# Column tiles or the full array for the dense matmuls behind the last attention times V

## The chip, the cores and the metric

The kernel runs on one core of one Trainium2 chip. The metric is the device time of one execution in microseconds, and the median of several runs is compared. The engines of the core are named as the profile names them: PE (TensorE, the matmuls; PEld are its weight loads), DVE (VectorE), ACT (ScalarE), POOL (GpSimd) and SP (SyncE, which issues the transfers).

## The reference

The input x has 2048 tokens of 512 features, in bf16. Two branches are computed from it and mixed by a gate per token.

- Branch A is attention in segments with a memory: 32 heads of 16 features, 4 segments of 512 tokens. Within a segment it is causal softmax attention. Beside that, each segment reads a memory matrix and a normaliser that the earlier segments have filled with phi(k) times v, where phi(t) is t + 1 for positive t and exp(t) otherwise. Both parts are mixed by a sigmoid per head, and the result is multiplied by wo.
- Branch B is a gated feed-forward layer: relu(x W_gate) times (x W_up), 1792 wide, times W_down.
- The output is g a + (1 - g) b, where g is a sigmoid of the sum of x times gate_w.

Cut to what matters here:

```
q, k, v = x @ wq, x @ wk, x @ wv          # heads of 16, segments of 512
o = g_h * memory(q) + (1 - g_h) * softmax(q k^T / 4 + mask) v
a = o @ wo
h = relu(x @ W_gate) * (x @ W_up)          # 2048 x 1792
b = h @ W_down
out = g * a + (1 - g) * b
```

## The kernel before

**How the work is tiled.** A segment is 512 tokens. Activations lie transposed in SBUF, features on the 128 partitions and the 512 tokens of a segment along the free axis. Per segment the kernel does four chunks each of q and k (proj_q, proj_k), four of v (proj_v), the scores and their exponentials (visit), the masks, attention times V (in attention), the read of the memory (dens and recall) and its update (memory), and the feed-forward layer (ffn_tasks): 14 chunks of gate and up, whose product is kept in 14 tiles hT, and then four output tiles of 128 tokens each (out_tile). An output tile gathers in one PSUM bank 14 matmuls of hT times wd_sb and 4 matmuls of oT times wo_sb. oT is the attention result, transposed. DVE multiplies the bank by a column ngcol into osr (line 958), and SP issues the transfer to the output (line 966).

**The last output tile** (tt = 15) is cut in three parts of columns: 256, 128 and 128 wide, each with its own 18 matmuls, its own eviction and a bank of its own. The first two parts take banks 7 or 6 (OBANKS), the third bank 5 or 4. The first part is written out alone, the other two together.

**Two ways to use the array.** The attention matmuls have small operands and use parts of the array. A score matmul contracts over 32 rows; these tasks have mode "row" (line 683). Attention times V, the denominators and the memory update write 32 output rows; they have mode "col" (lines 755, 812 and 878) and issue four matmuls that lie side by side in the array's columns. The read of the memory uses 32 by 32 tiles, mode "quad" (line 853). The dense matmuls (projections, feed-forward, output) have no mode. They contract over 128 rows and write 128, and full() can issue each of them in two ways:

```
if not col:
    nc.tensor.matmul(out, lhsT=lhsT, rhs=rhs, start=start, stop=stop)      # line 491
    return
for j in range(4):                                                       # line 495, four times
    r = slice(32 * j, 32 * j + 32)
    nc.tensor.matmul(out[r], lhsT=lhsT[:, r], rhs=rhs, ..., tile_position=(0, 32 * j))
```

A dense task has up to two matmuls (GM = 2). Its field flex holds their number if the matmul is wider than 128 columns, and 0 otherwise. So the dense tasks of the 128-wide parts of the last output tile can never be column-tiled, since their flex is 0.

**What sets the order.** Every operation is a task of a plan. The list ORDER, written out in the file, gives the order in which all tasks are issued, and UNITS gives the buffer that each takes. The plan's dependencies are only looked at by an assertion, that a task stands behind those it depends on. The waits between engines come from the tiles that the instructions read and write. Each engine works off its own instructions in the order of the list.

**Which way a dense task goes** is set in Plan.run by settle(). The PE tasks between two row or quad tasks make a stretch. If there is a col task anywhere in the stretch, all dense tasks of it with flex over 0 are column-tiled; if there is none, all use the full array. The last stretch of the program begins behind the last scores. It holds the last two attention times V tasks, the last gate and up chunks of segment 3 and all matmuls of the output tiles 12 to 15.

Of the kernel before, what the change touches and what calls it, by code (L numbers as in the profile page):

```python
# [12 lines left out]
P = 128  # L13
# [5 lines left out]
NSEG = 4  # L19
# [111 lines left out]
class Plan:  # L131
# [19 lines left out]
    def run(self):  # L151
        order = [self.tasks[int(n)] for n in ORDER.split()]
        slots = {}
        for t in self.tasks:
            for s in t.need + t.frees:
                slots.setdefault(id(s), s)
        assert len(order) == len(set(map(id, order))) == len(self.tasks)
        assert len(slots) == len(UNITS)
        for s, n in zip(slots.values(), UNITS):
            s.units = s.cands[int(n, 36)]  # L160
        for t in self.tasks:
            for s in t.frees:
                s.left += 1
        stretch, held, done = [], set(), set()

        def settle():
            col = any(t.mode == "col" for t in stretch)
            for t in stretch:
                t.col = bool(t.flex) and col
            stretch.clear()  # L170
        for t in order:
            assert all(d.n in done for d, off in t.deps if off % 1 != 0.25)
            done.add(t.n)
            for s in t.need:
                assert not held & set(s.units)
                held |= set(s.units)
            if t.eng == "PE":
                if t.mode in ("row", "quad"):
                    settle()
                else:  # L180
                    stretch.append(t)
            for s in t.frees:
                s.left -= 1
                if s.left == 0:
                    held -= set(s.units)
        settle()
        return order


@with_exitstack  # L190
def kernel(
# [71 lines left out]
    def bank(slot):  # L263
        return ps[:, slot.i * L:(slot.i + 1) * L]
# [165 lines left out]
    att, prj, ffn, xread, x0_first = {}, {}, {}, [], []  # L430
# [58 lines left out]
    def full(out, lhsT, rhs, start, stop, col):  # L489
        if not col:  # L490
            nc.tensor.matmul(out, lhsT=lhsT, rhs=rhs, start=start, stop=stop)  # L491
            return
        for j in range(4):
            r = slice(32 * j, 32 * j + 32)
            nc.tensor.matmul(out[r], lhsT=lhsT[:, r], rhs=rhs, start=start, stop=stop,  # L495
                             tile_position=(0, 32 * j))

    def matmuls(key, deps, sl, ops, start=True, stop=True, prev=None, width=L, need=(), chunk={}, at=0):
        n = len(ops)
        for k in range(0, n, GM):  # L500
            def emit(col=False, k=k):
                for q in range(k, min(k + GM, n)):
                    lhsT, rhs = ops[q]()
                    full(bank(sl)[:, at:at + width], lhsT, rhs, start and q == 0,
                         stop and q == n - 1, col)
            first = prev is None
            m = min(k + GM, n) - k
            t = plan.add("PE", (width / 2.4 + 2.5) * m, key - (0 if first else CONT), emit,
                         list(deps) + [d for q in range(k, k + m) for d in chunk.get(q, ())],
                         PEL, need=[sl] + list(need) if first else (),  # L510
                         flex=m if width > P else 0, size=2 * m)
            if not first:
                t.deps.append((prev, 0.0))
            prev, deps = t, ()
        return prev
# [397 lines left out]
    def ffn_tasks(seg):  # L913
        plan.tag = "gu"
        i = seg % 2
        hs = []
        for fv in range(NF):
            key = K(4 * seg + FLAG + fv * 4.0 / 18)
            gsl, usl, rs, hs1 = work(), work(), plan.one("rgr"), plan.one("hT")
            piece = next(k for k, (a, b) in enumerate(FP) if a <= fv * P < b)  # L920
            g = matmuls(key, xin(seg) + [got_g[piece]], gsl, proj_mm(wg_sb, fv, seg),
                        need=[rs])
            r = plan.add("ACT", 478, key - RL, lambda sl=gsl, rs=rs: nc.scalar.activation(  # L923
                rgr[rs.i][:], bank(sl), ACT.Relu), [g], ACL, frees=[gsl])
            u = matmuls(key + 1, xin(seg) + [got_u[piece]], usl, proj_mm(wu_sb, fv, seg),
                        need=[hs1])
            xread.extend((g, u))
            hs.append((plan.add("DVE", 605, key - RL, lambda sl=usl, rs=rs, hs1=hs1: (
                nc.vector.tensor_tensor(hT[hs1.i][:], bank(sl), rgr[rs.i][:], ALU.mult)),  # L929
                [r, u], DVL, frees=[usl, rs]), hs1))  # L930
        for qb in range(4):
            tt = 4 * seg + qb
            key = K(4 * seg + FLAG + (14 + qb) * 4.0 / 18)
            parts = [[(0, D)]]
            if tt == NT - 1:
                parts = [[(0, 2 * P)], [(2 * P, 3 * P), (3 * P, D)]]
            for cols in parts:
                out_tile(seg, i, hs, key, qb * P, tt, cols)

    def out_tile(seg, i, hs, key, lc, tt, cols):  # L940
        plan.tag = "down"
        os, b, c0 = plan.one("osr"), [], cols[0][0]
        for n0, n1 in cols:
            w = n1 - n0
            sl = plan.one("ps", [HOST] if tt < 12 else OBANKS if n0 < 3 * P else (5, 4))
            prev, mine = None, []
            for f0, f1 in ((0, 5), (5, 10), (10, 14)):
                prev = matmuls(key, [h[0] for h in hs[f0:f1]] + got_d[0:2 if f0 < 5 else 4]
                               + [att["ot", 4 * seg + c] for c in range(OTW)], sl, [
                    lambda fv=fv, n0=n0, n1=n1: (hT[hs[fv][1].i][:, lc:lc + P], wd_sb[:, fv, n0:n1])  # L950
                    for fv in range(f0, f1)], start=(f0 == 0), stop=False, prev=prev, width=w)
                prev.frees += tuple(h[1] for h in hs[f0:f1])
                mine.append(prev)
            a = matmuls(key, got_o + [att["ot", 4 * seg + c] for c in range(NC)], sl, [
                lambda ci=ci, n0=n0, n1=n1: (oT[i][:, ci, lc:lc + P], wo_sb[:, ci, n0:n1])
                for ci in range(NC)], start=False, prev=prev, width=w)
            b.append(plan.add("DVE", 95 + 1.12 * w, key - RL, lambda sl=sl, n0=n0, n1=n1: (
                nc.vector.tensor_scalar(osr[os.i][:, n0 - c0:n1 - c0], bank(sl)[:, 0:n1 - n0],  # L958
                                        ngcol[:, tt:tt + 1], None, ALU.mult)),
                [a, att["ng", seg]] + b, DVL, need=[] if b else [os], frees=[sl]))  # L960
            if tt < 12:
                first = mine[0].deps[-1][0].deps[-1][0]
                hosts.append((first, a))
        ffn["o", seg, tt % 4] = a
        c1 = cols[-1][1]
        plan.add("SP", 400, key, lambda: nc.sync.dma_start(
            out=outf[tt * P:(tt + 1) * P, c0:c1], in_=osr[os.i][:, 0:c1 - c0]), b[-1:],
            1400 if tt == NT - 1 else 2400, frees=[os], xfer=400.0)
# [101 lines left out]
```

## Time and profile before

| what | value |
|---|---|
| median of 3 runs | 263.6 us (263.37 to 263.92) |
| the profiled execution's own time | 262.86 us |
| its span, first to last instruction | 261.1 us |
| PE busy | 257.4 us, 4137 matmuls |
| DVE, ACT, POOL busy | 202.1, 182.9, 67.3 us |
| mean granted TensorE clock | 1.0 of full |

The profile shows one execution. Its page gives the busy time of each engine and the chain of work that ended last. The timeline lists instructions in order of time, neighbours of one line, operation and tiles merged into a row: start, length, engine, line, operation, written and read tiles, array rows by array columns used, moving columns, and the count. Matmuls overlap in the array, so the length of a row holds the drain of its last matmul, and the difference between the starts of two rows is what the first costs the stream. Shapes of a merged row are those of its first instruction.

### The profile page before, as it was taken

What the parts mean: (1) busy time and instruction counts of PE and PEld (TensorE: products, weight loads), DVE (VectorE), ACT (ScalarE), POOL (GpSimd) and SP (SyncE); (2) the same over time, 40 slices, a digit from 0 to 9 for tenths busy, and PEclk for the clock granted to TensorE, in tenths of its full rate; (3) what the DMA queues carried; (4) which work ended last, traced back from release to release, by engine and by line L of the source; (5) the groups of instructions that cost most, each with busy time, mean ns of one, the idle gap of its engine ahead of it and who ended that gap; (6) DMA issues with size and microseconds to landing.
All of it is one profiled execution on the core that took longest, in us unless ns stands there. A gap on an engine that the chain in (4) does not pass through costs nothing.

```text
span 261.1 us, 9476 instructions
## 1 busy us (share of the span) xinstructions
PE 257.4 (99%) x4137; PEld 120.3 (46%) x4137; DVE 202.1 (77%) x452; ACT 182.9 (70%) x186; POOL 67.3 (26%) x188
## 2 busy tenths in 40 slices
PE   8999999999999999999999999999999999999995
PEld 3434444445445544444545444444445544455443
DVE  1699889998979957998998874887988736586521
ACT  2299899999889668888296848999278856891000
POOL 8028651423313113121030423123022322111000
DMA  7999881120006335000026440000000043000011
GB/s 186 335 290 259 264 195 48 19 62 3 3 25 151 104 52 125 18 3 3 15 55 120 138 143 20 4 3 15 4 1 13 20 147 92 0 3 5 3 43 40
DMA packets 31601, 19.76 MB, mean 76 GB/s; under 512 B 16072, under 2 KB 30024, under 8 KB 31560
## 3 DMA queue, kind: packets, MB, share of 16 engines
q1 hardware_dynamic: 31144, 18.90, 28.1%
q8 instruction: 32, 0.52, 0.8%
q10 hardware_dynamic: 416, 0.26, 0.3%
q14 instruction: 9, 0.07, 0.1%
HBM read 13.21 MB, written 2.55 MB: 60 GB/s over the span
## 4 chain that ended last, share of the span: by engine, by line
PE 98%; ACT 0%; DVE 0%; issue 0%
PE ps L491 50%; PE ps L495 30%; PE ps L683 9%; PE ps L755 7%; PE ps L1003 1%; PE ps L878 1%; PE ps L853 0%; PE ps L812 0%; PE ps L529 0%; ACT xT L544 0%; DVE osr L958 0%
## 5 line engine op out<-in xcount | busy, mean ns | idle before, releaser
L712 ACT ACTIVATE E<-ps 128x2048 bf16<-128x2048 f32 (+3 forms) x79 | 120.4, 1552 | 26.4 <-PE ps L683 25.6
L728 POOL TENSOR_SCALAR_AFFINE_SELECT E<-E 128x256 bf16<-128x256 bf16 x128 | 53.7, 448 | 155.0 <-ACT E L712 149.1
L929 DVE TENSOR_TENSOR hT<-ps,rgr 128x512 bf16<-128x512 f32 x56 | 37.8, 681 | 21.9 <-PE ps L491 13.6
L923 ACT ACTIVATE rgr<-ps 128x512 bf16<-128x512 f32 x56 | 32.7, 597 | 20.4 <-PE ps L495 8.9
L491 PE MATMUL ps<-xT,wu_sb 128*128 128x512 bf16 x164 | 43.0, 380 | 0.0
L491 PE MATMUL ps<-xT,wg_sb 128*128 128x512 bf16 x136 | 35.5, 380 | 0.0
L495 PE MATMUL ps<-wd_sb,hT 128*32 128x512 bf16 (+1 forms) x572 | 33.9, 369 | 0.0
L683 PE MATMUL ps<-QT,KT 32*128 32x64 bf16 (+3 forms) x768 | 27.8, 244 | 0.0
L786 DVE STREAM_TRANSPOSE T<-ps 128x512 f32<-128x512 f32 x32 | 21.9, 700 | 3.6 <-PE ps L755 3.2
L495 PE MATMUL ps<-xT,wg_sb 128*32 128x512 bf16 x352 | 23.7, 380 | 0.0
L491 PEld LDWEIGHTS <-wu_sb 128*128 128x128 bf16 x164 | 14.9, 98 | 18.5 <-issue 2.5
L491 PE MATMUL ps<-wd_sb,hT 128*128 128x512 bf16 (+1 forms) x109 | 23.0, 340 | 0.0
L683 PEld LDWEIGHTS <-KT 32*128 32x128 bf16 x768 | 11.0, 92 | 24.2 <-issue 22.9
L958 DVE TENSOR_SCALAR osr<-ps,ngcol 128x512 bf16<-128x512 f32 (+2 forms) x18 | 12.3, 682 | 12.5 <-PE ps L495 9.7
L491 PEld LDWEIGHTS <-wg_sb 128*128 128x128 bf16 x136 | 12.7, 98 | 15.7 <-issue 1.3
L495 PEld LDWEIGHTS <-hT 128*32 128x32 bf16 x572 | 14.0, 97 | 13.0 <-issue 1.3
L755 PE MATMUL ps<-E,Vp 128*17 128x320 bf16 (+3 forms) x512 | 19.1, 273 | 0.0
L712 ACT ACTIVATE Em<-ps 128x2048 bf16<-128x2048 f32 (+2 forms) x11 | 15.6, 1415 | 4.3 <-PE ps L683 4.1
L495 PE MATMUL ps<-xT,wu_sb 128*32 128x512 bf16 x240 | 16.2, 379 | 0.0
L491 PE MATMUL ps<-wv_sb,xT 128*128 128x512 bf16 x58 | 14.7, 380 | 0.0
L586 DVE CAST QT<-ps 128x512 bf16<-128x512 f32 x16 | 10.8, 683 | 4.9 <-PE ps L491 4.5
L491 PE MATMUL ps<-xT,wk_sb 128*128 128x512 bf16 x52 | 14.0, 380 | 0.0
(100 smaller groups left out, 306.9 us busy)
## 6 DMA issues: line engine op xcount, KB each, us to landing
out_dram<-osr SPq DMA_DIRECT2D x15, 128.0 KB
xn<-in_A_x_dram SPq DMA_DIRECT2D x3, 512.0 KB
xn<-coefs SPq DMA_DIRECT2D x6, 256.0 KB
cdr<-coefs SPq DMA_DIRECT2D x6, 256.0 KB
wg_sb<-in_B_W_gate_dram SPq DMA_DIRECT2D x2, 512.0 KB
wu_sb<-in_B_W_up_dram SPq DMA_DIRECT2D x2, 512.0 KB
wd_sb<-in_B_W_down_dram SPq DMA_DIRECT2D x2, 512.0 KB
wg_sb<-in_B_W_gate_dram SPq DMA_DIRECT2D x2, 384.0 KB
```

The costliest lines, as they stand in the source:

```text
L491: nc.tensor.matmul(out, lhsT=lhsT, rhs=rhs, start=start, stop=stop)
L495: nc.tensor.matmul(out[r], lhsT=lhsT[:, r], rhs=rhs, start=start, stop=stop, tile_position=(0, 32 * j))
L586: prj["q", seg, c] = plan.add("DVE", 600, key - RQK, lambda: nc.vector.tensor_copy(QT[i][:], bank(sl)), [a] + war, DVL, frees=[sl])
L683: nc.tensor.matmul(ps[:, o:o + w], lhsT=lhsT.rearrange("p h q -> p (h q)"), rhs=rhs, start=True, stop=True, tile_position=(32 * j, 0))
L712: lambda n0=n0, n1=n1, u=u, f=f, j0=j0, j1=j1: nc.scalar.activation(target(u, f, j0, j1), ps[:, banks[n0] * L:(banks[n0] + n1 - n0) * L], ...
L728: nc.gpsimd.affine_select(out=m[:, :, o:o + HP], in_=m[:, :, o:o + HP], compare_op=ALU.is_ge, fill=0.0, base=HP, pattern=[[0, 4], [1, HP]] ...
L755: nc.tensor.matmul(bank(sl)[32 * m:32 * m + HW, q:q + w], lhsT=(Vp[i] if n < 4 else Vm)[:, kb, r, 4 * c + j, 0:HW], rhs=rhs, start=(n == 0 ...
L786: done.append(plan.add("DVE", 633, key - RL, lambda r=r, sl=sl: nc.vector.transpose(T[ts.i][:, r], bank(sl)), [a] + done, 75 if r else 0, ...
L878: nc.tensor.matmul(bank(sl)[32 * j:32 * j + 32, 34 * g:34 * g + 34], lhsT=pK[i][:, t, g * P + 32 * j:g * P + 32 * j + 32], rhs=Vp[i][:, t, ...
L923: r = plan.add("ACT", 478, key - RL, lambda sl=gsl, rs=rs: nc.scalar.activation(rgr[rs.i][:], bank(sl), ACT.Relu), [g], ACL, frees=[gsl])
L929: nc.vector.tensor_tensor(hT[hs1.i][:], bank(sl), rgr[rs.i][:], ALU.mult)),
L958: nc.vector.tensor_scalar(osr[os.i][:, n0 - c0:n1 - c0], bank(sl)[:, 0:n1 - n0], ngcol[:, tt:tt + 1], None, ALU.mult)),
```

## The change

settle() now finds the places of the col tasks in a stretch. Up to the last of them nothing is different: dense tasks with flex are column-tiled. Behind the last one, dense tasks stay column-tiled until the first task that has no flex, and from there to the end of the stretch all dense tasks use the full array. A stretch without a col task uses the full array, as before.

The second edit adds a dependency to the tasks of the parts of the last output tile that are at most 128 wide: they stand behind the last attention times V of the program (task "pv" 15).

```diff
         def settle():
-            col = any(t.mode == "col" for t in stretch)
-            for t in stretch:
+            cols = [n for n, t in enumerate(stretch) if t.mode == "col"]
+            col = bool(cols)
+            for n, t in enumerate(stretch):
+                col = col and (bool(t.flex) or n <= cols[-1])
                 t.col = bool(t.flex) and col
             stretch.clear()
...
                 prev = matmuls(key, [h[0] for h in hs[f0:f1]] + got_d[0:2 if f0 < 5 else 4]
+                               + ([(att["pv", 4 * NSEG - 1], 0.0)] if w <= P else [])
                                + [att["ot", 4 * seg + c] for c in range(OTW)], sl, [
```

ORDER and UNITS are the same. The lines behind the edits move down by two or three.

## The prediction

> **What bounds the kernel now.** I read the page first, for which engine sets the end.
>
> ```profile
> span 261.1 us, 9476 instructions
> PE 257.4 (99%) x4137; PEld 120.3 (46%) x4137; DVE 202.1 (77%) x452; ACT 182.9 (70%) x186; POOL 67.3 (26%) x188
> PE 98%; ACT 0%; DVE 0%; issue 0%
> PE ps L491 50%; PE ps L495 30%; PE ps L683 9%; PE ps L755 7%; PE ps L1003 1%; PE ps L878 1%; PE ps L853 0%; PE ps L812 0%; PE ps L529 0%; ACT xT L544 0%; DVE osr L958 0%
> ```
>
> PE is busy 99% of the span, and the chain that ended last is 98% PE. So a nanosecond taken from PE's stream near the end is a nanosecond of the span, unless a wait takes its place. L491 is a dense matmul on the full array, L495 the same matmul as four column tiles. The change touches only the choice between these two lines, so the second view is the timeline of PE behind the last attention times V. The columns are start, length (with the drain of the last one), engine, line, operation, tiles, shape and count; the difference between two starts is what a piece costs the stream.
>
> ```profile
> 242.20 0.60 PE L495 MATMUL ps<-xT,wu_sb 128*32 128x512 bf16 x8
> 242.74 0.40 PE L491 MATMUL ps<-wd_sb,hT 128*128 128x128 bf16 x4
> 243.07 0.61 PE L495 MATMUL ps<-xT,wg_sb 128*32 128x512 bf16 x8
> 243.51 3.41 PE L495 MATMUL ps<-wd_sb,hT 128*32 128x512 bf16 x60
> 246.75 1.04 PE L495 MATMUL ps<-wo_sb,oT 128*32 128x512 bf16 x16
> 247.61 1.04 PE L495 MATMUL ps<-wd_sb,hT 128*32 128x512 bf16 x16
> 248.47 1.04 PE L495 MATMUL ps<-wo_sb,oT 128*32 128x512 bf16 x16
> 249.34 2.33 PE L495 MATMUL ps<-wd_sb,hT 128*32 128x512 bf16 x40
> 251.60 0.23 PE L491 MATMUL ps<-wd_sb,hT 128*128 128x128 bf16 x1
> 251.76 1.26 PE L495 MATMUL ps<-wd_sb,hT 128*32 128x512 bf16 x24
> 252.85 1.04 PE L495 MATMUL ps<-wo_sb,oT 128*32 128x512 bf16 x16
> 253.82 0.28 PE L491 MATMUL ps<-wd_sb,hT 128*128 128x128 bf16 x2
> 254.04 0.73 PE L495 MATMUL ps<-wd_sb,hT 128*32 128x256 bf16 x20
> 254.70 0.29 PE L491 MATMUL ps<-wd_sb,hT 128*128 128x128 bf16 x2
> 254.91 0.51 PE L495 MATMUL ps<-wd_sb,hT 128*32 128x256 bf16 x12
> 255.36 0.45 PE L491 MATMUL ps<-wd_sb,hT 128*128 128x128 bf16 x5
> 255.74 0.62 PE L495 MATMUL ps<-wd_sb,hT 128*32 128x256 bf16 x16
> 256.30 0.56 PE L491 MATMUL ps<-wd_sb,hT 128*128 128x128 bf16 x7
> 256.79 0.62 PE L495 MATMUL ps<-wo_sb,oT 128*32 128x256 bf16 x16
> 257.34 0.34 PE L491 MATMUL ps<-wd_sb,hT 128*128 128x128 bf16 x3
> 257.52 0.39 PE L491 MATMUL ps<-wo_sb,oT 128*128 128x128 bf16 x4
> 257.74 0.39 PE L491 MATMUL ps<-wd_sb,hT 128*128 128x128 bf16 x4
> 257.97 0.39 PE L491 MATMUL ps<-wo_sb,oT 128*128 128x128 bf16 x4
> ```
>
> The reader is to see that the stream changes between the two lines thirteen times here: seven times into L491, six times back. PE waits for nothing in it. The clean unit prices are these. A group of four column tiles 512 wide: from 243.51 to 246.75, 15 groups in 3.24, 0.216 us each. A full matmul 128 wide: 257.52 to 257.97, 8 in 0.45, 0.056 each. A group 256 wide: the row at 251.76 holds four groups of 512 and two of 256 (the grouping names the first shape only), 1.09 - 4 x 0.216 = 0.23 for two, 0.109 to 0.113 each.
>
> **The change part by part.**
>
> The rule in settle. Behind the last column task of a stretch, dense tasks keep column tiles until the first task that can't have them, and then use the full array. Tasks that can't are those at most 128 wide, and those exist only for the last output tile. So the only place where the program changes is behind 242.74, the first four 128-wide matmuls. From there 47 groups of 512 (8 + 60 + 16 + 16 + 16 + 40 + 16 + 16 in the rows, divided by 4) and 18 groups of 256 (8 + 20 + 12 + 16 + 16, divided by 4) become 65 full matmuls: 195 matmuls and 195 weight loads fewer on PE. No other engine's order, no wait, no bank and no transfer changes.
>
> The price of a 512-wide matmul, full against four tiles. The full one is seen in the dense stretch before the last attention work:
>
> ```profile
> 212.45 1.03 PE L491 MATMUL ps<-xT,wg_sb 128*128 128x512 bf16 x4
> 213.31 1.03 PE L491 MATMUL ps<-xT,wu_sb 128*128 128x512 bf16 x4
> 214.18 0.59 PE L491 MATMUL ps<-wo_sb,oT 128*128 128x512 bf16 x2
> L491 PEld LDWEIGHTS <-wg_sb 128*128 128x128 bf16 x14 | 1.3, 98 | 1.6 <-issue 0.2
> ```
>
> 213.31 to 214.18 is 0.87 for four, 212.45 to 213.31 is 0.86: 0.216 each, as the group of four tiles. So 47 conversions cost and bring nothing. The 98 ns weight loads (last row) lie under the stream.
>
> The price of a full 256-wide matmul isn't in the trace. Its lower bound is half of a 512-wide one, 0.108; its upper bound is what the column group costs, 0.113. I take 0.109, on the line between 0.056 at 128 and 0.216 at 512. The 18 together are then uncertain by 0.1 us at most, and I count them as equal to their groups. That a load of 98 ns could show under a stream of 109 is excluded by the 128-wide ones, which have the same load and run at 56.
>
> The changes of mode. Each piece, less its matmuls at the unit prices, leaves what the change costs. Into the full array: 249.34 to 251.60 is 2.26 for ten groups, 0.10 over; 252.85 to 253.82 is 0.97 for four, 0.11 over; the next four (254.04, 254.91, 255.74, 256.79) are 0.115, 0.12, 0.12 and 0.115 over. Back into tiles: 242.74 to 243.07 is 0.33 for four of 0.056, 0.106 over; 251.60, 253.82, 254.70, 255.36 and 256.30 are 0.10, 0.11, 0.10, 0.10 and 0.10 over. The one into the full array ahead of 242.74 stays (242.20 to 242.74 is 0.54 for two groups, 0.11 over). The other twelve go. As a check in one sum: from 242.74 to 257.97 are 15.23 us; 32 x 0.056 + 47 x 0.216 + 18 x 0.109 = 13.91; the difference is 1.32. Of it 0.01 stays, since the piece behind any change runs 0.01 longer. PE ends 1.31 earlier. The bounds are 12 x 0.10 = 1.2 and 12 x 0.12 = 1.44.
>
> What of this lies beside other work: nothing, PE is alone on the path. But the neighbours get less time, and each has to be asked:
>
> ```profile
> 244.36 0.69 DVE L929 TENSOR_TENSOR hT<-ps,rgr 128x512 bf16<-128x512 f32 x1
> 245.71 0.42 DVE L771 TENSOR_TENSOR oT<-oT,omr 128x512 bf16<-128x512 bf16 x1
> 253.94 0.75 DVE L958 TENSOR_SCALAR osr<-ps,ngcol 128x512 bf16<-128x512 f32 x1 [3.63 <-PE ps L495]
> 257.46 0.48 DVE L958 TENSOR_SCALAR osr<-ps,ngcol 128x256 bf16<-128x256 f32 x1 [2.77 <-PE ps L495]
> 258.39 0.35 DVE L958 TENSOR_SCALAR osr<-ps,ngcol 128x128 bf16<-128x128 f32 x1
> 258.77 0.33 SPq L966 DMA_DIRECT2D out_dram<-osr  x1
> 258.80:259.20 0.40, 0.00 (x0) 0.00 (x0) 0.00 (x0) 0.00 (x0) 0.00 (x0) 1.00 0.58 163
> 259.60:260.00 0.40, 0.00 (x0) 0.00 (x0) 0.00 (x0) 0.00 (x0) 0.00 (x0) 1.00 0.59 163
> ```
>
> The last hT is there at 245.05 and the last oT at 246.13; the first wo matmul of tile 12 stands at 246.75 and moves to 246.64. Covered by 0.5 us. The bank of tile 14 is reused by the third part of the last tile at 255.36. Its eviction starts at 253.94, 0.44 behind the start of the last wo matmul of that tile (252.85 + 3 x 0.216 = 253.50), and is done 1.19 behind it. After the change PE comes to the reuse 0.216 + 2 x 0.056 + 5 x 0.109 + 2 x 0.056 + 3 x 0.109 = 1.31 behind it, where it is 1.86 now. So 0.67 us of cover shrinks to 0.12, less the 0.06 that a release takes from PE to DVE (253.50 + 0.38 of drain to 253.94). It holds, narrowly; I count nothing. The end: counted from the start of the last 256-wide wo matmul (256.79 + 3 x 0.109 = 257.12), the three evictions need 0.34 + 0.48 + 0.35 to come to the last one, 1.17, and PE lets it go at 0.109 + 14 x 0.056 + 0.23 (the drained length at 251.60) + 0.03 (257.97 + 0.39 to 258.39) = 1.15. DVE now binds by 0.02 instead of PE. The two last output transfers, 0.24 us of traffic each in the last two rows (0.58 and 0.59 of 0.40), move from 0.80 apart to about 0.70: still apart.
>
> The added dependency on the last attention times V orders the 128-wide matmuls in the plan; the order is a written list and keeps it already, so it issues nothing and costs nothing.
>
> The sum: -1.31 + 0.02 = -1.29, about -1.3. The profiled execution took 262.86 us (its span 261.1 and 1.8 around it), so it would be 261.6. The median of the three runs shown is 263.6, 0.7 over the profiled one; the forecast of the median is 263.6 - 1.3 = 262.3, 0.5% faster.
>
> **The rivals.**
>
> The reuse wait. If the eviction of tile 14 is seen later than the 0.06 left over, PE stalls at the third part. The row at 253.94 speaks for it by its narrowness; a stall longer than 0.2 us is hard to make of it. It would leave -1.1: 262.5.
>
> The cost isn't the mode's. If the 0.11 hung on the change of width (512 to 128 and back) and not on the change of tiling, the same twelve would stay: 263.6, no change. Against it: the row at 251.76 goes from 512 to 256 and back to 512 within column tiles at 0.01 over its parts. For it: no row goes from 512 to 128 within the full array.
>
> The full weight loads come out from under the stream; this one ends on the other side. Today the tail loads 32 columns at a time; afterwards 65 loads of 128 columns follow each other. If all 98 ns of each were seen, that is 65 x 0.098 = 6.4, less 1.3: 268.7. It turns the sign from 1.3 / 65 = 20 ns a matmul. Against it: 0.216 at 212.45 with such loads. The Trainium skill, TensorE: Matmul & The Clock Gate, Part 3, under what overlaps and what doesn't, states this rule: a weight load overlaps matmuls in flight only when its row group differs, which for full-height operands it never does. By that rule the sum would be the 268.7 of this rival, and the trace contradicts it at 512 and at 128 wide; only 256 wide is unseen.
>
> **How the numbers follow.** Forecast 0.76, reuse wait 0.09, cost not the mode's 0.09, weight loads 0.06. Under 0.2% (0.5 us) this kernel can't be told from no change. Faster is the first two, with a little off for run spread: 0.85; same 0.09; slower 0.06. The range holds the first two: from 263.37, the lowest run, less 1.44, 261.9, to 263.92, the highest, less 1.1, 262.8; since the profiled execution lies 0.5 under the lowest run, I add 0.4 below and 0.2 above: 261.5 to 263.0.
>
> **What would show it.** Right: behind the first four 128-wide matmuls no L495 row is left (renumbered by two lines), 256-wide rows at 0.109, and from that piece to the last matmul 13.9 us instead of 15.2, with everything ahead as before. A gap on PE ahead of the five 128-wide matmuls, ended by osr, would show the first rival; steps of 0.1 between 512 and 128 wide, the second; a 512-wide pitch over 0.216, the third. The forecast is wrong if the stream ahead of 242.7 runs differently, for which the program gives no reason.

## The result and the profile after

| | before | changed |
|---|---|---|
| median | 263.44 us (263.31 to 263.92, 6 runs) | 262.06 us (261.48 to 262.61, 6 runs) |
| ratio | | 0.9944, 95% interval 0.9927 to 0.9961 |
| profiled execution, its span | 262.86 us, 261.1 us | 262.61 us, 260.9 us |

The changed kernel is 0.56% faster, about 1.4 us of 263.4. The forecast was 262.3 and 0.5%. But the two profiled executions are only 0.25 us apart, so the first thing to clear up is where the rest of the gain is in them. The page of the changed kernel:

```profile
span 260.9 us, 9058 instructions
PE 254.1 (97%) x3914; PEld 120.7 (46%) x3942; DVE 202.1 (77%) x452; ACT 183.0 (70%) x186; POOL 67.3 (26%) x188
PE 97%; issue 1%; DVE 0%
PE ps L493 53%; PE ps L497 25%; PE ps L685 9%; PE ps L757 7%; PE ps L1006 1%; PE ps L880 1%; PE ps L855 0%; PE ps L531 0%; PE ps L814 0%; DVE osr L961 0%; PE ps L540 0%
```

Lines have moved by two or three: L493 is the full array now, L497 the column tiles. The share of the chain that lies in tiles fell from 30% to 25%. Weight loads fell from 4137 to 3942, by the 195 that were forecast. Of the matmuls, 28 records are missing in this trace (3914 beside 3942 loads, where before has 4137 of both), so counts and busy times of matmuls aren't compared; starts are. The timeline of PE behind the last attention times V:

```profile
243.81 0.40 PE L493 MATMUL ps<-wd_sb,hT 128*128 128x128 bf16 x4
244.26 0.38 PE L493 MATMUL ps<-xT,wg_sb 128*128 128x512 bf16 x1
244.48 3.40 PE L493 MATMUL ps<-wd_sb,hT 128*128 128x512 bf16 x15
247.72 1.03 PE L493 MATMUL ps<-wo_sb,oT 128*128 128x512 bf16 x4
...
250.31 3.46 PE L493 MATMUL ps<-wd_sb,hT 128*128 128x512 bf16 x17
253.60 1.03 PE L493 MATMUL ps<-wo_sb,oT 128*128 128x512 bf16 x4
254.46 2.37 PE L493 MATMUL ps<-wd_sb,hT 128*128 128x128 bf16 x28
256.67 0.60 PE L493 MATMUL ps<-wo_sb,oT 128*128 128x256 bf16 x4
257.10 0.33 PE L493 MATMUL ps<-wd_sb,hT 128*128 128x128 bf16 x3
...
257.72 0.39 PE L493 MATMUL ps<-wo_sb,oT 128*128 128x128 bf16 x4
```

The alternation is gone. From the first 128-wide matmul to the last row are 257.72 - 243.81 = 13.91 us, where before has 257.97 - 242.74 = 15.23: 1.32 less. The unit prices are those that before showed: 15 matmuls in 3.24 from 244.48 to 247.72, 0.216 each; and four 256-wide ones from 256.67 to 257.10, 0.1075 to two decimals of the starts.

So the whole forecast gain is in this stretch, and the stretch began 1.07 us later, at 243.81 and not 242.74. That delay is there already in the first microseconds. The timeline of PE at the first q and k projections, and the stretch from 4.5 to 7.5 us in the view by windows (columns: length, busy time of PE, PEld, DVE, ACT, POOL with counts, granted clock, DMA share, GB/s), of before:

```profile
4.61 1.89 PE L491 MATMUL ps<-xT,wq_sb 128*128 128x512 bf16 x8
6.33 1.89 PE L491 MATMUL ps<-xT,wk_sb 128*128 128x512 bf16 x8
238.84 0.61 PE L755 MATMUL ps<-E,Vp 128*17 128x448 bf16 x16
4.50:7.50 3.00, 2.89 (x14) 1.43 (x15) 0.24 (x1) 0.33 (x2) 1.80 (x13) 1.00 1.17 265
```

and of the changed kernel:

```profile
4.57 3.00 PE L493 MATMUL ps<-xT,wq_sb 128*128 128x512 bf16 x8
7.41 1.89 PE L493 MATMUL ps<-xT,wk_sb 128*128 128x512 bf16 x8
239.92 0.61 PE L757 MATMUL ps<-E,Vp 128*17 128x448 bf16 x16
4.50:7.50 3.00, 3.00 (x11) 1.25 (x10) 0.28 (x1) 0.39 (x2) 1.80 (x13) 1.00 1.14 270
```

The same eight q matmuls take 6.33 - 4.61 = 1.72 us in one execution and 7.41 - 4.57 = 2.84 in the other; PE is busy in both and does 14 matmuls in 3 us in one and 11 in the other: in before all q matmuls start 0.216 us apart, in the changed kernel's execution the first five intervals are 0.40 to 0.43. The instructions there are the same in both kernels. From the first k matmul to the last attention times V group both need the same: 238.84 - 6.33 = 232.51 and 239.92 - 7.41 = 232.51. The totals carry this start; the stretch behind it doesn't. The experiments are therefore read in four pieces: the start (to the first k projection matmul), the middle (from there to the last 448-wide group of attention times V), the stretch (from there to the last matmul) and the end.

### The profile page after: what moved, and what is told of

Read it like the earlier page. It is cut to its first block, busy times and chain, and to the rows that moved or that the text cites. A ratio compares the mean times of both kernels' runs of the same rounds, so it can differ in the third digit from the quotient of the medians.

```text
span 260.9 us, 9058 instructions
## 1 busy us (share of the span) xinstructions
PE 254.1 (97%) x3914; PEld 120.7 (46%) x3942; DVE 202.1 (77%) x452; ACT 183.0 (70%) x186; POOL 67.3 (26%) x188
## 4 chain that ended last, share of the span: by engine, by line
PE 97%; issue 1%; DVE 0%
PE ps L493 53%; PE ps L497 25%; PE ps L685 9%; PE ps L757 7%; PE ps L1006 1%; PE ps L880 1%; PE ps L855 0%; PE ps L531 0%; PE ps L814 0%; DVE osr L961 0%; PE ps L540 0%
## 5 line engine op out<-in xcount | busy, mean ns | idle before, releaser
L493 PE MATMUL ps<-xT,wu_sb 128*128 128x512 bf16 x158 | 41.9, 380 | 0.6 <-issue 0.5
L493 PE MATMUL ps<-xT,wg_sb 128*128 128x512 bf16 x132 | 34.9, 379 | 0.6 <-issue 0.3
L493 PE MATMUL ps<-wd_sb,hT 128*128 128x512 bf16 (+2 forms) x147 | 29.5, 339 | 1.4 <-issue 1.3
L497 PE MATMUL ps<-wd_sb,hT 128*32 128x512 bf16 x384 | 24.0, 380 | 0.0
L493 PEld LDWEIGHTS <-wu_sb 128*128 128x128 bf16 x164 | 14.9, 98 | 18.5 <-issue 2.5
L497 PE MATMUL ps<-xT,wg_sb 128*32 128x512 bf16 x344 | 23.1, 380 | 0.0
L493 PEld LDWEIGHTS <-wg_sb 128*128 128x128 bf16 x138 | 12.9, 98 | 15.7 <-issue 1.3
L493 PEld LDWEIGHTS <-hT 128*128 128x128 bf16 x156 | 13.5, 98 | 14.1 <-issue 2.3
L497 PE MATMUL ps<-xT,wu_sb 128*32 128x512 bf16 x240 | 16.2, 379 | 0.0
L493 PE MATMUL ps<-xT,wq_sb 128*128 128x512 bf16 x49 | 14.3, 407 | 0.2 <-issue 0.2
L493 PE MATMUL ps<-wv_sb,xT 128*128 128x512 bf16 x54 | 13.9, 379 | 0.4 <-issue 0.3
```

## The experiments

The theory: a matmul on the full array costs what its four column tiles cost, and PE pays some 0.11 us for each change of tiling, so that twelve changes fewer are the whole gain. The rivals: tiles are dearer as such (1.32 us over 65 conversions, 0.020 each); the price is the change of width; the full weight loads show.

**The width** needs no run. In the changed kernel the row at 250.31 goes from 512 to 128, back to 512 and to 256 wide, all on the full array: 253.60 - 250.31 = 3.29, and 14 x 0.216 + 0.056 + 2 x 0.109 = 3.30 (14, 1 and 2 of them by the program's order). There is no room in it for steps of 0.1.

**Six tasks put back into tiles.**

```diff
-            col = bool(cols)
+            col, late = bool(cols), 0
...
                 t.col = bool(t.flex) and col
+                if cols and not col and t.flex:
+                    late += 1
+                    t.col = late in (3, 6, 9, 12, 15, 18)
```

> Edit: in the changed kernel, behind the first 128-wide matmuls, six dense tasks of the 512-wide ones (10 of 47 groups) are put back into column tiles, each with full matmuls on both sides, so that there are again twelve changes of tiling. Same stretch as above. Theory (a change of tiling costs 0.1 to 0.12): 17.97 + 12 x 0.11 = 19.29, the whole gain lost, and the time as before. Rival (tiles dearer as such): 17.97 + 10 x 0.020 = 18.17, and the time 0.2 us over the changed kernel's.

PE's timeline of this kernel, two of the six places and both ends of the stretch:

```profile
240.18 0.61 PE L760 MATMUL ps<-E,Vp 128*17 128x448 bf16 x16
...
245.26 0.40 PE L500 MATMUL ps<-wd_sb,hT 128*32 128x512 bf16 x4
245.59 1.04 PE L496 MATMUL ps<-wd_sb,hT 128*128 128x512 bf16 x4
246.56 0.40 PE L500 MATMUL ps<-wd_sb,hT 128*32 128x512 bf16 x4
246.89 0.82 PE L496 MATMUL ps<-wd_sb,hT 128*128 128x512 bf16 x3
...
259.30 0.39 PE L496 MATMUL ps<-wo_sb,oT 128*128 128x128 bf16 x4
```

From the group at 240.18 to the last matmul (259.30 + 3 x 0.056 = 259.47) are 19.29 us, as before's 258.14 - 238.84 = 19.30; the changed kernel has 257.89 - 239.92 = 17.97. One group in tiles between full matmuls takes 245.59 - 245.26 = 0.33 and not 0.216, and the four full ones behind it 0.97 and not 0.86: 0.11 for each change. Ten of 65 conversions taken back cost all of the gain. Tiles dearer as such would have cost 0.2; that rival falls. The time was 263.23 us (262.91 to 264.19, 10 runs) beside 263.67 of before (263.16 to 264.05, 15 runs), a ratio of 0.9985, 0.9975 to 0.9994: near before, as expected. The 0.4 us between the medians are not in the stretch, and where they are stays open.

**One part alone: the 256-wide ones stay in tiles.**

```diff
-                t.col = bool(t.flex) and col
+                t.col = bool(t.flex) and (col or bool(cols) and t.dur < 150 * t.flex)
```

> Edit: in the changed kernel the 256-wide dense matmuls stay in column tiles, so that only the 47 of 512 are converted; behind the first 128-wide matmuls ten of the twelve changes of tiling remain. Stretch from the last attention times V group to the last matmul. Theory (only the changes cost): 17.97 + 10 x 0.11 = 19.07. Rival (tiles dearer as such, 0.020 each): 17.97 + 18 x 0.020 = 18.33.

```profile
239.76 0.61 PE L757 MATMUL ps<-E,Vp 128*17 128x448 bf16 x16
...
258.66 0.39 PE L493 MATMUL ps<-wo_sb,oT 128*128 128x128 bf16 x4
```

The stretch is 258.66 + 0.17 - 239.76 = 19.07, to the hundredth what ten changes make of it. Converting 47 matmuls with two changes fewer brought 0.22 of the 1.32. The total, 263.55 us in its one run, lies over the 262.94 of before's run beside it; in its trace the start is late, at 7.24 us (the table below).

**The full array directly behind the last column task.**

```diff
-                col = col and (bool(t.flex) or n <= cols[-1])
+                col = bool(cols) and n <= cols[-1]
```

> Edit: the dense matmuls use the full array directly behind the last attention times V, without staying in tiles up to the first 128-wide one; 15 more groups are converted and the number of changes of tiling stays one. Measured from the start of the last 448-wide attention times V group to the start of the last matmul, where before has 19.29 us and the changed kernel 17.97. Theory (only a change of tiling costs, 0.1 us each, and a full matmul costs as much as its four tiles): 17.97, within 0.02. Rival (column tiles are dearer as such, the 1.32 us spread over the 65 converted groups, 0.020 each): 15 more of them, 17.67. Rival (the weight loads of full matmuls come out from under the stream): over 17.97.

PE's timeline of this kernel, with one row of its weight loads:

```profile
6.43 1.89 PE L493 MATMUL ps<-xT,wk_sb 128*128 128x512 bf16 x8
11.03 1.41 PEld L493 LDWEIGHTS <-xT 128*128 128x128 bf16 x8 [0.40 <-DMA wv_sb<-in_A_wv_dram]
58.06 1.48 PE L497 MATMUL ps<-xT,wg_sb 128*32 128x512 bf16 x24
59.36 0.67 PE L880 MATMUL ps<-Vp,pK 128*32 128x34 bf16 x64
60.19 0.38 PE L493 MATMUL ps<-xT,wg_sb 128*128 128x512 bf16 x1 [0.16 <-issue]
60.51 0.40 PE L685 MATMUL ps<-QT,KT 32*128 32x320 bf16 x8
...
240.58 0.61 PE L757 MATMUL ps<-E,Vp 128*17 128x448 bf16 x16
...
258.38 0.39 PE L493 MATMUL ps<-wo_sb,oT 128*128 128x128 bf16 x4
```

and the same place in before:

```profile
57.67 1.48 PE L495 MATMUL ps<-xT,wg_sb 128*32 128x512 bf16 x24
58.97 0.67 PE L878 MATMUL ps<-Vp,pK 128*32 128x34 bf16 x64
59.47 0.63 PE L495 MATMUL ps<-xT,wg_sb 128*32 128x512 bf16 x8
60.02 0.40 PE L683 MATMUL ps<-QT,KT 32*128 32x320 bf16 x8
```

The stretch is 258.38 + 0.17 - 240.58 = 17.97: fifteen more groups converted with no change of tiling fewer brought nothing, as the theory has it. What the expectation had not counted is the middle, 240.58 - 6.43 = 234.15 where before has 232.51. This form of the rule acts in every stretch. Fifteen earlier ones end in dense work in tiles before the next row or quad task; there PE now goes from tiles to the full array and then to row tiles, one change more. In the rows, tiles to scores take 60.51 - 58.06 = 2.45 and not 60.02 - 57.67 = 2.35. (The idle 0.16 in the row at 60.19 stands where the record of the first of two matmuls is missing.) Of the 1.64 in all, 0.07 are not tiling: the v projection starts that much later than in before, counted from the first k matmul, since its weights wv_sb land late (the row at 11.03). Fifteen such places make the other 1.57, 0.105 each. The total, 263.28 us in its one run, gives back all that the stretch had won. So the detail of the change, to stay in tiles until a task that can't, is worth some 1.6 us against the simpler rule: in the earlier stretches no such task comes, and they stay as they were.

**No change of tiling at all in the last stretch.** In the kernel before, the 128-wide ones may use tiles too:

```diff
-                       flex=m if width > P else 0, size=2 * m)
+                       flex=m, size=2 * m)
```

> Edit: in the kernel before, the 128-wide matmuls may be column-tiled too, so that the whole stretch behind the last attention times V is in tiles and no change of tiling is left in it. Same stretch as above. Theory (only the changes cost): one change fewer than in the changed kernel, 17.97 - 0.12 = 17.85, if a 128-wide group of four takes the 0.056 of a full one; the nearest row, 64-wide groups of attention times V at 0.029, speaks for that. If the four tiles and four loads of such a group can't be issued that fast, each of the 36 groups shows it. Rival (tiles dearer as such, 0.020 a group): 19.29 - 13 x 0 + 36 x 0.020 = 20.0. The time by the theory: 1.4 us below before, 0.1 below the changed kernel.

> The kernel with the whole last stretch in tiles once more, for one profile. In its first one the last output transfer's issue on SP took 0.86 us where the others have 0.33, and the end behind the last matmul 3.56 where they have 3.01. If that goes with this program, it is there again; if it is a chance of that execution, the end is 3.0. The stretch 17.865 again.

PE's and SP's timelines of the first of these two executions, SP's of the second, and SP's of the changed kernel run beside the first:

```profile
239.61 0.61 PE L755 MATMUL ps<-E,Vp 128*17 128x448 bf16 x16
...
257.30 0.40 PE L495 MATMUL ps<-wo_sb,oT 128*32 128x128 bf16 x16
258.12 0.86 SPq L966 DMA_DIRECT2D out_dram<-osr  x1
```

```profile
257.99 0.73 SPq L966 DMA_DIRECT2D out_dram<-osr  x1
```

```profile
257.40 0.33 SPq L969 DMA_DIRECT2D out_dram<-osr  x1
```

The last matmul group starts at 257.30 + 3 x 0.056 = 257.47, and the stretch is 17.86, 0.11 under the changed kernel's: the thirteenth change is gone, and a 128-wide group in tiles costs the 0.056 of a full matmul. That is the theory once more, from the other side: the gain needs no full array, only one tiling. But the kernel was not the fastest: 262.75 us (262.05 to 262.8, 5 runs) beside 263.67 of before, ratio 0.9961, 0.9948 to 0.9973, and beside 261.57 of the changed kernel in the same session. The expectation had 1.4 us below before; the medians are 0.9 apart. Part of the distance to the changed kernel is the start, which in its profile was late (7.10 us to the first k matmul, against 6.28 in the changed kernel's). Part is its own: the last output transfer's issue took 0.86 and 0.73 us in its two profiles and 0.33 in the eight others. It goes with this program, then, and makes the end 3.56 and 3.44 us long where the others have 3.01 or 3.02. Its last 15 groups issue eight instructions (four loads, four matmuls) per 0.056 us. In both of its traces a packet of an instruction queue (q8) is still being moved when that issue starts: from 257.50 to 258.61 us beside the issue at 258.12, and from 257.14 to 258.34 beside the issue at 257.99; the issue ends 0.37 and 0.38 us behind the packet. In the eight others the last such packet ends before the issue starts (in the changed kernel's two, 0.77 and 0.28 us before). That the issue waits for the packet was not tested and stays open.

**The changed kernel again, and before again.**

> The changed kernel once more, beside the others on one chip. Same stretch: 17.97 again, to 0.02. The time 1.3 us below before. The spread of its runs: if the 1.07 us by which its first profile was late already at 8.8 us come from the moment at which the matmuls leave the slow pace of the first microseconds, then the profiles of these four kernels differ in that moment by up to some 3 us, in all later PE work ahead of the tail by nothing, and each total is the moment's delay plus a constant.

> The kernel before once more, for one profile. The stretch 19.29, and the time from the first k projection matmul to the last attention times V group 232.51, as in its first profile and in those of the changed kernel. If the totals vary by what lies ahead of and behind that work, this profile's total differs from 262.86 by as much as its first k projection differs from 6.33 us and its last stretch behind the last matmul from 3.01, and by nothing else. If the kernel before had a later start or a longer end than the changed one, beside its slower stretch, both of its profiles would have to show it; the first has neither.

> The kernel before a third time, for one profile: as the one before it. If the issue of the last transfer is slow now and then in programs whose last matmuls are in tiles, two more profiles of such a program beside the one just asked for should show 0.86 at least once.

| profile | total | start | middle | stretch | end |
|---|---|---|---|---|---|
| before, first | 262.86 | 6.33 | 232.51 | 19.29 | 3.01 |
| before, second | 263.14 | 6.61 | 232.51 | 19.29 | 3.02 |
| before, third | 264.04 | 6.80 | 233.22 | 19.29 | 3.02 |
| changed, first | 262.61 | 7.41 | 232.51 | 17.97 | 3.01 |
| changed, second | 261.57 | 6.28 | 232.51 | 17.97 | 3.02 |
| six tasks back | 264.19 | 6.67 | 233.51 | 19.29 | 3.02 |
| 256-wide in tiles | 263.55 | 7.24 | 232.51 | 19.07 | 3.02 |
| full array at once | 263.28 | 6.43 | 234.15 | 17.97 | 3.02 |
| all in tiles, first | 262.75 | 7.10 | 232.51 | 17.86 | 3.56 |
| all in tiles, second | 262.56 | 6.90 | 232.58 | 17.86 | 3.44 |

The stretch repeats to 0.01 us; the start varies by 1.1 us, not by up to the 3 of the expectation, and has no side: it was latest and earliest in the changed kernel. The second profile of before differs from its first by 0.28 in total and by 0.28 in the start. The third holds 0.71 in the middle that the expectation had not allowed for, all of it before 13 us, where the inputs arrive. Its timeline names the transfer:

```profile
6.80 1.90 PE L491 MATMUL ps<-xT,wk_sb 128*128 128x512 bf16 x8
10.09 1.47 PE L491 MATMUL ps<-xT,wk_sb 128*128 128x512 bf16 x6 [0.51 <-DMA wk_sb<-in_A_wk_dram]
240.02 0.61 PE L755 MATMUL ps<-E,Vp 128*17 128x448 bf16 x16
```

The run with six tasks put back holds 1.00 more in its middle, all of it before 23 us: two waits there are for late transfers (wv_sb and xT), one is for an exponential.

In the second session the changed kernel had 261.57 us (261.48 to 262.04, 5 runs), a ratio of 0.9927, 0.9915 to 0.994, which is 1.9 us, more than the stretch can give: its 1.32 are 0.9950, just outside the interval. Since the stretch repeats to 0.01 us in all profiles, the missing 0.6 should lie ahead of it or behind it. The kernel with six tasks back, whose stretch is before's, was also 0.4 faster than before in that session, so most of the 0.6 need not have to do with the change. The start and the loads vary by enough, about a microsecond; but of the unprofiled runs no trace tells, and the cause stays open.

## Why the prediction was right

The mechanism and nearly each term came out as stated.

- The conversions, costed at nothing: 47 at 0.216 and 18 at 0.109. Right; two runs show it apart from the changes of tiling. With the full array at once, 15 groups more are converted at the changed kernel's number of changes, and the stretch is the same 17.97; with six tasks back, 55 are converted at before's number of changes, and it is before's 19.29.
- The changes of tiling, twelve at 0.10 to 0.12: 13.9 us forecast from the first 128-wide matmul to the last row, 13.91 measured; 1.31 forecast, 1.32 measured. Twelve put back and ten left in had the same price, 0.11 each; the fifteen added elsewhere had 0.105.
- The unseen price, a full 256-wide matmul: taken as 0.109, the line between two widths; four from 256.67 to 257.10.
- The reuse of tile 14's bank: no stall. DVE in the changed kernel:

```profile
254.67 0.75 DVE L961 TENSOR_SCALAR osr<-ps,ngcol 128x512 bf16<-128x512 f32 x1 [3.41 <-PE ps L493]
257.31 0.48 DVE L961 TENSOR_SCALAR osr<-ps,ngcol 128x256 bf16<-128x256 f32 x1 [1.89 <-PE ps L493]
257.71 0.34 DVE L961 TENSOR_SCALAR osr<-ps,ngcol 128x128 bf16<-128x128 f32 x1
258.14 0.35 DVE L961 TENSOR_SCALAR osr<-ps,ngcol 128x128 bf16<-128x128 f32 x1
```

  The eviction ends at 255.42, and the third part begins, in the rhythm of the row at 254.46, 1.31 behind 254.25, at 255.56: a cover of 0.14, where the sum gave 0.12.
- The end: the sum let DVE bind by 0.02. It doesn't. The second eviction starts 0.40 behind the first (257.31, 257.71), not 0.48, since neighbours on DVE overlap a little; the last waits for PE's last matmul (257.72 + 0.39) as before, and the end is 3.01 in both. It starts 1.15 behind the last 256-wide matmul (256.67 + 3 x 0.1075 = 256.99), which is PE's term of the sum. The 0.02 for DVE were wrong.
- The base: the forecast took the median shown. That the profiled execution lay 0.5 under the lowest run was left unexplained there; the start, early in that execution, and late loads in others make gaps of this size, though no trace of those runs shows it.
- The slower rival, weight loads that show, fell with the first 0.216 behind 244.48: 98 ns loads of 128 columns stay hidden at 512, 256 and 128 wide. The rule that the Trainium skill states on TensorE: Matmul & The Clock Gate, Part 3, that loads overlap matmuls in flight only when their row groups differ, doesn't hold for these streams; the trace has full-height loads under full-height matmuls without a gap.

## What to carry to other kernels

Count changes of tiling, not tiles: on PE's path each one costs about 0.11 us here, at all the widths seen (128 to 512 columns), while a dense matmul costs the same on the full array as in four column tiles of 32. Choose the tiling of flexible work by its neighbours on both sides, and look at the few pieces that can't follow (here the 128-wide ones), since each breaks the run twice. Measure such an edit in the stretch of the trace that it touches, from one fixed instruction to another: here that repeats to 0.01 us, while totals vary by a microsecond for other reasons.

## What the runs showed of the hardware that was not expected

The moment at which matmuls leave the slow pace of the start differs between executions of the same instructions: eight 512-wide matmuls from 4.6 us on took 1.72 us in one and 2.84 in another, and this alone moves the total by 1.1 us. The granted clock in the view by windows is 1.00 in both, so that view doesn't show it; the starts of the matmuls do. The Trainium skill, TensorE: Matmul & The Clock Gate, Part 1, says that the clock gate opens after a window of some 3.4 us that runs freely and isn't reset by the kernel's start. The spread of 1.1 us agrees with that; no run here tests it.

A change of tiling costs 0.10 to 0.12 us not only into and out of column tiles. From the full array to the row tiles of the scores it is 0.10 too, here in before: two matmuls of 0.216 and then a start 0.53 behind the first.

```profile
214.61 0.59 PE L491 MATMUL ps<-xT,wu_sb 128*128 128x512 bf16 x2
215.14 0.40 PE L683 MATMUL ps<-QT,KT 32*128 32x320 bf16 x8
```

And a program whose last groups are all in small tiles had its last transfer issued in 0.73 and 0.86 us, not 0.33, on another engine's queue.
